# Splitting the first weight load of a transfer-bound decode kernel: 8 KB runs first, 24 KB runs last

## The chip, the cores and the metric

The kernel runs on one core of one Trainium2 chip. The metric is the device time of one execution in microseconds (us), median of several. A "run" of bytes (8 KB runs) is a contiguous stretch that a transfer moves as one packet; idle time in "engine-us" is summed over the sixteen DMA engines. The profile is one execution; its span is some 1.3 us shorter than the device time of the same execution. A "kernel before" always ran on the same chip beside the kernel it is compared with. Ratios are the mean time of one kernel's runs over that of the other's of the same rounds, so they are not quite the ratio of the medians quoted beside them.

## The reference

One decode step of an attention mixer beside an MLP, mixed by a gate, for batch 8, one token, width 576:

```
q = x @ wq                                  # wq: 576 x 4096, 32 heads of 128
k, v = the last 2048 of 8192 cached rows    # 16 kv heads, each used by two q heads
a = softmax(q k^T / sqrt(128)) v @ wo
b = gelu(layernorm(x) @ w1 + b1) @ w2 + b2
g = sigmoid(sum(x * gate_w))
out = g * a + (1 - g) * b
```

Nearly all of its work is reading: K and V are 67 MB each, the four weights 20 MB together.

## The kernel before

A plan lists all operations with what they depend on, a small cost model puts them in order for each engine, and that order is emitted. All large loads are issued by SP (SyncE) one after the other, in a fixed sequence. The parts that matter:

```python
# the first loads (SP), in this order; the weights wq and w1 share the K/V buffer slots
d_wqr = dma("sp", ... (wq_r, A_wq[512:576, :].rearrange("k (s c) -> (k s) c", s=2)), "wq", ...)       # 0.5 MB, 4 KB runs
d_wqm = dma("sp", ... (wq_m..., A_wq[0:512, :].rearrange("(p t) c -> p (t c)", t=4)), "wq", ...)      # 4.2 MB, 32 KB runs
dwq = [d_wqm, d_wqr]
d_w1m = dma("sp", ...)                                                                                # 4.7 MB, 36 KB runs
d_w1r = dma("sp", ...)                                                                                # 0.6 MB
# ... cut: q_fn multiplies xT by wq_m and wq_r and waits for dwq ...
# the sequence of the other loads: a number is a K load (4.2 MB), v a V load (2.1 MB), w wo, m w2
order = ("0 1 v 2 v 3 v 4 v v 5 v v 6 v v 7 v v 8 v v 9 v v 10 v v 11 v v 12 v v 13 v v 14 v 15 "
         "w w v v w w v v v v v v b m m m m")
# a K load waits until the K load two before it has been transposed (DVE), as it takes its buffer
slot_free[s] = trs
# ... cut ...
# at the end: the first two SP issues (and one of ACT) are moved ahead of the start barrier
for etype, count in ((mybir.EngineType.SP, 2), (mybir.EngineType.Activation, 1)):
```

Of the kernel before, what the change touches and what calls it, by code (L numbers as in the profile page):

```python
# [38 lines left out]
class _Plan:  # L39
# [16 lines left out]
    def dma(self, eng, fn, semkey, nbytes, deps=(), name=None, after=(), prio=0):  # L56
        op = _Op(eng, fn, deps, name, self.DMA_ISSUE, after=after, is_dma=True, dma_sem=semkey, nbytes=nbytes, prio=prio)
        op.idx = len(self.all)
        self.all.append(op)
        return op  # L60
# [108 lines left out]


ARENA_BASE = 16512


def held_matmul(nc, e, out, lhsT, rhs, start=False, stop=True, skip=False, tile_size=(128, 128), tile_position=(0, 0)):
    return e.add_instruction(mybir.InstMatmult(
        name=nc.get_next_instruction_name(), engine=mybir.EngineType.PE,
        ins=[e.lower_ap(rhs), e.lower_ap(lhsT)], outs=[e.lower_ap(out)],
        start_tensor_calc=start, stop_tensor_calc=stop, is_transpose=False, bass_skip_group_check=skip,
        tile_size=tile_size, tile_position=tile_position, ldweights=False))


def build_kernel(nc, A_x, A_k_cache, A_v_cache, A_wq, A_wo, B_x, B_w1, B_b1, B_w2, B_b2, gate_w, out):
# [24 lines left out]
    with ExitStack() as es:  # L207
# [126 lines left out]
        wq_m = RAW[:, WQO:WQO + 4 * 4096].rearrange("p (t c) -> p t c", t=4)  # L334
        wq_r = RAW[:, WQO + 4 * 4096:WQO + 4 * 4096 + 2048]
# [22 lines left out]
        add, dma = P.add, P.dma  # L358
# [26 lines left out]
        d_b1 = dma("act", lambda e: e.dma_start(b1c, B_b1.rearrange("(c f) -> c f", c=FC)), "b", F * 2, name="d_b1", after=[d_gw])  # L385
        dx = [d_x, d_gw, d_gw1]
        db = [d_b1]
        d_wqr = dma("sp", lambda e: e.dma_start(wq_r, A_wq[512:576, :].rearrange("k (s c) -> (k s) c", s=2)), "wq", 64 * 8192, name="d_wqr")
        d_wqm = dma("sp", lambda e: e.dma_start(wq_m.rearrange("p t c -> p (t c)"), A_wq[0:512, :].rearrange("(p t) c -> p (t c)", t=4)), "wq", 512 * 8192, name="d_wqm", after=[d_wqr])
        dwq = [d_wqm, d_wqr]  # L390
        d_w1m = dma("sp", lambda e: e.dma_start(w1_m.rearrange("p t c -> p (t c)"), B_w1[0:512, :].rearrange("(p t) c -> p (t c)", t=4)), "w1", 512 * F * 2, name="d_w1m", after=[d_wqm])
        d_w1r = dma("sp", lambda e: e.dma_start(w1_r, B_w1[512:576, :].rearrange("k (s c) -> (k s) c", s=2)), "w1", 64 * F * 2, name="d_w1r", after=[d_w1m])
        dw1 = [d_w1m, d_w1r]
# [173 lines left out]
        count = {"K": 0, "V": 0, "W": 0, "M": 0, "B": 0}  # L567
# [266 lines left out]
        handles = {"sp": nc.sync, "act": nc.scalar, "pool": nc.gpsimd, "dve": nc.vector, "pe": nc.tensor}  # L834
        for eng in ENGS:
            P.emit(eng, handles[eng], eng_sems, dma_sems)
        for etype, count in ((mybir.EngineType.SP, 2), (mybir.EngineType.Activation, 1)):
            first = [i for i in entry[n_entry:] if i.engine == etype][:count]
            assert all(isinstance(i, mybir.InstDMACopy) for i in first)
            for i in first:  # L840
                entry.remove(i)
            at = next(n for n, i in enumerate(entry) if i.engine == etype and isinstance(i, mybir.InstDrain))
            entry[at:at] = first
# [4 lines left out]
def bass_gated_mix__sliding_block_cached__mixer_channel_mlp__decode_kernel(  # L848
    nc: bass.Bass,
    A_x: bass.AP,  # L850
    A_k_cache: bass.AP,
    A_v_cache: bass.AP,
    A_wq: bass.AP,
    A_wo: bass.AP,
    B_x: bass.AP,
    B_w1: bass.AP,
    B_b1: bass.AP,
    B_w2: bass.AP,
    B_b2: bass.AP,
    gate_w: bass.AP,  # L860
    out: bass.AP,
):
    build_kernel(nc, A_x, A_k_cache, A_v_cache, A_wq, A_wo, B_x, B_w1, B_b1, B_w2, B_b2, gate_w, out)
# [28 lines left out]
```

## Time and profile before

| | kernel before |
|---|---|
| device time | 366.29 us (366.27 to 366.82, 3 runs) |
| span of the profile | 364.9 us |
| bytes read | 154.31 MB, 423 GB/s over the span |
| DMA queue of SP | 98.9% of sixteen DMA engines |
| DVE, PE busy | 62%, 66% |

The table says that the sixteen DMA engines are the bound: what does not make them start sooner, run faster or end more evenly does not show in the time. The lines themselves are in the prediction.

### The profile page before, as it was taken

The numbers are of one execution on the slowest core, as the hardware profiler recorded it, in microseconds if no ns is written. First come the engines' busy times: TensorE is split into PE (matmuls) and PEld (weight loads), VectorE is DVE, ScalarE is ACT, GpSimd is POOL, SyncE is SP. The second block draws the span as 40 slices with busy tenths as digits, with TensorE's granted clock in tenths as the row PEclk, the third lists the DMA queues.
The fourth block names the chain that finished last, engine by engine and source line by source line (L and its number), as shares of the span: only waits on it lengthen the run. The fifth ranks groups of instructions, "written<-read, shape, count | busy, mean of one in ns | idle before, by whom it ended". The sixth has DMA issues, their size and how long they took to land.

```text
span 364.9 us, 3980 instructions
## 1 busy us (share of the span) xinstructions
PE 239.4 (66%) x1679; PEld 115.0 (32%) x1679; DVE 226.5 (62%) x340; ACT 22.4 (6%) x53; POOL 17.4 (5%) x80
## 2 busy tenths in 40 slices
PE   0269684838498938274959484738959297577575
PEld 0159331312143414022423232214424133234232
DVE  4700995675999280759965362789781739777221
ACT  1010000000000000000100000001100000001000
POOL 5021000001000000010000000000000000000000
PEclk9999998778589969596996978676978796859899
DMA  9999999999999999999999999999999999999995
GB/s 376 435 404 451 406 451 411 451 432 415 445 426 443 420 436 431 424 438 424 436 426 440 422 442 420 439 422 438 424 436 444 426 410 436 425 431 429 431 425 222
DMA packets 9690, 154.58 MB, mean 424 GB/s; under 512 B 1052, under 2 KB 1220, under 8 KB 2888
## 3 DMA queue, kind: packets, MB, share of 16 engines
q1 hardware_dynamic: 9616, 154.29, 98.9%
q8 instruction: 13, 0.21, 0.2%
q10 hardware_dynamic: 56, 0.03, 0.0%
q14 instruction: 5, 0.04, 0.0%
HBM read 154.31 MB, written 0.01 MB: 423 GB/s over the span
## 4 chain that ended last, share of the span: by engine, by line
DMA 62%; DVE 24%; PE 11%; issue 1%; SPq 0%; DVEq 0%
DMA arena<-in_A_k_cache_dram 54%; DVE arena L666 18%; PE ps L678 6%; DMA arena<-in_A_v_cache_dram 5%; PE ps L711 4%; DMA arena<-in_B_w_dram 4%; DVE arena L639 3%; DVE arena L597 1%; DVE arena L631 1%; DVE arena L600 0%; DVE arena L606 0%; PE ps L612 0%; DVE arena L614 0%; PE ps L555 0%; SPq L798 0%
## 5 line engine op out<-in xcount | busy, mean ns | idle before, releaser
L666 DVE STREAM_TRANSPOSE arena<-arena 128x4096 f32<-128x4096 f32 x32 | 140.7, 4424 | 85.4 <-DMA arena<-in_A_k_cache_dram 85.0
L678 PE MATMUL ps<-arena 128*32 128x512 bf16 x512 | 141.7, 440 | 62.7 <-DVE arena L666 62.7
L678 PEld LDWEIGHTS ps<-arena 128*32 128x32 bf16 x512 | 52.3, 105 | 144.7 <-DVE arena L666 67.7
L711 PE MATMUL ps<-arena 128*32 128x512 bf16 x512 | 60.7, 453 | 23.8 <-DVE arena L602 18.6
L711 PEld LDWEIGHTS ps<-arena 128*32 128x32 bf16 x512 | 24.8, 110 | 50.4 <-issue 31.7
L639 DVE STREAM_TRANSPOSE arena<-arena 128x512 bf16<-128x512 bf16 x32 | 30.8, 1019 | 0.0
L728 PE MATMUL ps<-arena 128*128 128x16 f32 x128 | 17.0, 264 | 5.6 <-ACT arena L722 3.9
L761 DVE COPY arena<-arena 32x4 bf16<-32x4 bf16 (+1 forms) x80 | 12.9, 161 | 10.1 <-POOL arena L749 7.9
L728 PEld LDWEIGHTS ps<-arena 128*128 128x128 f32 x128 | 15.5, 191 | 11.5 <-ACT arena L722 9.6
L722 ACT ACTIVATE arena<-ps 128x512 f32<-128x512 f32 x16 | 9.6, 598 | 148.9 <-PE ps L711 148.9
L749 POOL TENSOR_TENSOR arena<-arena 128x8 bf16<-128x8 f32 x30 | 5.9, 231 | 229.9 <-ACT arena L738 229.9
L597 DVE TENSOR_REDUCE arena<-ps 128x1 f32<-128x512 f32 x8 | 5.5, 692 | 12.2 <-PE ps L678 12.1
L510 PE MATMUL ps<-arena 128*128 128x8 bf16 x144 | 10.9, 201 | 2.6 <-DMA arena<-in_B_w_dram 2.6
L608 ACT ACTIVATE arena<-ps,arena 128x512 bf16<-128x512 f32 x8 | 5.5, 687 | 107.4 <-DVE arena L606 107.4
L510 PEld LDWEIGHTS ps<-arena 128*128 128x128 bf16 x144 | 10.8, 157 | 3.1 <-DMA arena<-in_B_w_dram 3.1
L555 PE MATMUL ps<-arena 128*8 128x288 bf16 (+1 forms) x140 | 9.3, 288 | 3.6 <-DMA arena<-in_B_w_dram 3.4
L659 POOL TENSOR_TENSOR arena<-arena 128x32 bf16<-128x32 bf16 x32 | 6.5, 240 | 86.0 <-PE ps L678 76.9
L612 PE MATMUL ps<-arena 128*128 128x32 f32 x16 | 3.9, 328 | 8.6 <-DVE arena L611 8.6
L631 DVE TENSOR_SCALAR arena<-arena 128x512 bf16<-128x512 bf16 x32 | 9.0, 324 | 0.0
L425 PE MATMUL ps<-arena 8*128 8x8 bf16 x8 | 0.6, 170 | 11.0 <-DVE arena L398 7.0
L512 PE MATMUL ps<-arena 128*128 128x8 bf16 x36 | 7.2, 201 | 0.0
L555 PEld LDWEIGHTS ps<-arena 128*8 128x8 bf16 (+1 forms) x140 | 4.6, 85 | 7.8 <-DMA arena<-in_B_w_dram 4.9
(84 smaller groups left out, 77.8 us busy)
## 6 DMA issues: line engine op xcount, KB each, us to landing
arena<-in_A_k_cache_dram SPq DMA_DIRECT2D x16, 4096.0 KB, 25.2
arena<-in_A_v_cache_dram SPq DMA_DIRECT2D x32, 2048.0 KB, 24.3
arena<-in_B_w_dram SPq DMA_DIRECT2D x1, 4608.0 KB, 24.1
arena<-in_A_wo_dram SPq DMA_DIRECT2D x4, 1152.0 KB, 10.0
arena<-in_A_wq_dram SPq DMA_DIRECT2D x1, 4096.0 KB, 13.4
arena<-in_B_w_dram SPq DMA_DIRECT2D x3, 1296.0 KB, 18.9
arena<-in_B_w_dram SPq DMA_DIRECT2D x2, 432.0 KB, 12.2
arena<-in_B_w_dram SPq DMA_DIRECT2D x1, 576.0 KB, 25.2
```

Source lines behind the costliest of these rows:

```text
L510: ins = e.matmul(out_, lhsT, yT[:, kt, :], start=(kt == 0), stop=False)
L512: ins = e.matmul(out_, lhsT, yT[:, 4 + c // 2, :], start=False, stop=True)
L555: ins = e.matmul(ps[c:c + 8, BK_ACC, 0:JN], lhsT, rhs[:, JN * j:JN * j + JN], start=False, stop=True, skip_group_check=True, tile_position ...
L597: mx = add("dve", lambda e: e.tensor_reduce(out=k(MX), in_=ps[:, bank, :], axis=AXL.X, op=ALU.max), deps=[qk_done[g]], name="mx%d" % g, co ...
L631: return e.tensor_scalar(out=dst, in0=view("Pd").rearrange("p (s n) -> p s n", s=2), scalar1=amask[:, a:a + 1], scalar2=None, op0=ALU.mult)
L639: return e.transpose(dst, src)
L666: tr = add("dve", (lambda h=h, kb=kb: lambda e: e.transpose(bass.AP(arena_f, offset=foffs("KT") + kb * SE // 2, ap=[[AST // 2, 128], [4, 1 ...
L678: mm = e.matmul(ps[32 * c:32 * c + 32, 2 * (G % 2) + nb, :], qb[:, G % 2, n, 2 * h + ee, :], rhs, start=(h == 0 and t == 0), stop=(h == 1 ...
L711: mm = e.matmul(ps[c:c + 32, bk, :], PT[:, g % 2, 512 * q + 32 * t:512 * q + 32 * t + 32], slot(s)[:, 512 * t:512 * t + 512], start=(t < 2 ...
L722: u_ev[item] = add("act", lambda e: e.activation(out=EV[:, item % 2, :], in_=ps[:, bk, :].rearrange("p (r d j) -> p r j d", r=4, j=4), fun ...
L728: mm = e.matmul(ps[:, BK_S, OC + 16 * (item % 2):OC + 16 * (item % 2) + 16], EV[:, item % 2, 128 * r:128 * r + 128], i2[:, r, :, :].rearra ...
L761: return [add("dve", (lambda j=j, q=q: lambda e: e.tensor_copy(oT[32 * q:32 * q + 32, ch, j, bs], oN[32 * j:32 * j + 32, q, ch, bs]))(), d ...
```

## The change

The intent: let the first transfer carry more bytes for each descriptor, so that the DMA engines are fed sooner. The first load becomes one row in four of wq (1 MB in 8 KB runs), then comes the remainder of 64 rows, then the other three quarters in 24 KB runs. Three issues stand ahead of the start barrier, at which the engines wait for each other before they begin, in place of two. A helper that nothing called is removed.

```diff
-def held_matmul(nc, e, out, lhsT, rhs, ...):        (8 lines, cut)
...
-        d_wqr = dma("sp", lambda e: e.dma_start(wq_r, A_wq[512:576, :].rearrange("k (s c) -> (k s) c", s=2)), "wq", 64 * 8192, name="d_wqr")
-        d_wqm = dma("sp", lambda e: e.dma_start(wq_m.rearrange("p t c -> p (t c)"), A_wq[0:512, :].rearrange("(p t) c -> p (t c)", t=4)), "wq", 512 * 8192, name="d_wqm", after=[d_wqr])
-        dwq = [d_wqm, d_wqr]
+        wq_rows = A_wq[0:512, :].rearrange("(p t) c -> p t c", t=4)
+        d_wq0 = dma("sp", lambda e: e.dma_start(wq_m[:, 0, :], wq_rows[:, 0, :]), "wq", 128 * 8192, name="d_wq0")
+        d_wqr = dma("sp", ... as before ..., after=[d_wq0])
+        d_wqm = dma("sp", lambda e: e.dma_start(wq_m[:, 1:4, :].rearrange("p t c -> p (t c)"), A_wq[0:512, :].rearrange("(p t) c -> p (t c)", t=4)[:, 4096:16384]), "wq", 384 * 8192, name="d_wqm", after=[d_wqr])
+        dwq = [d_wqm, d_wqr, d_wq0]
...
-        for etype, count in ((mybir.EngineType.SP, 2), (mybir.EngineType.Activation, 1)):
+        for etype, count in ((mybir.EngineType.SP, 3), (mybir.EngineType.Activation, 1)):
```

More of the change, by code (lines that the diff above doesn't have):

```diff
@@ L171 @@
 ARENA_BASE = 16512
-def held_matmul(nc, e, out, lhsT, rhs, start=False, stop=True, skip=False, tile_size=(128, 128), tile_position=(0, 0)):
-    return e.add_instruction(mybir.InstMatmult(
-        name=nc.get_next_instruction_name(), engine=mybir.EngineType.PE,
-        ins=[e.lower_ap(rhs), e.lower_ap(lhsT)], outs=[e.lower_ap(out)],
-        start_tensor_calc=start, stop_tensor_calc=stop, is_transpose=False, bass_skip_group_check=skip,
-        tile_size=tile_size, tile_position=tile_position, ldweights=False))
 def build_kernel(nc, A_x, A_k_cache, A_v_cache, A_wq, A_wo, B_x, B_w1, B_b1, B_w2, B_b2, gate_w, out):
@@ L387, in build_kernel @@
         db = [d_b1]
-        d_wqr = dma("sp", lambda e: e.dma_start(wq_r, A_wq[512:576, :].rearrange("k (s c) -> (k s) c", s=2)), "wq", 64 * 8192, name="d_wqr")
-        d_wqm = dma("sp", lambda e: e.dma_start(wq_m.rearrange("p t c -> p (t c)"), A_wq[0:512, :].rearrange("(p t) c -> p (t c)", t=4)), "wq", 512 * 8192, name="d_wqm", after=[d_wqr])
-        dwq = [d_wqm, d_wqr]
+        wq_rows = A_wq[0:512, :].rearrange("(p t) c -> p t c", t=4)
+        d_wq0 = dma("sp", lambda e: e.dma_start(wq_m[:, 0, :], wq_rows[:, 0, :]), "wq", 128 * 8192, name="d_wq0")
+        d_wqr = dma("sp", lambda e: e.dma_start(wq_r, A_wq[512:576, :].rearrange("k (s c) -> (k s) c", s=2)), "wq", 64 * 8192, name="d_wqr", after=[d_wq0])
+        d_wqm = dma("sp", lambda e: e.dma_start(wq_m[:, 1:4, :].rearrange("p t c -> p (t c)"), A_wq[0:512, :].rearrange("(p t) c -> p (t c)", t=4)[:, 4096:16384]), "wq", 384 * 8192, name="d_wqm", after=[d_wqr])
+        dwq = [d_wqm, d_wqr, d_wq0]
         d_w1m = dma("sp", lambda e: e.dma_start(w1_m.rearrange("p t c -> p (t c)"), B_w1[0:512, :].rearrange("(p t) c -> p (t c)", t=4)), "w1", 512 * F * 2, name="d_w1m", after=[d_wqm])
```

## The prediction

> **What bounds the kernel now.** I read the page first, its slices and its queue table, then the chain that ended last, then the DMA queue's own waits, then the windows of the first and last microseconds.
>
> ```profile
> span 364.9 us, 3980 instructions
> ...
> DMA  9999999999999999999999999999999999999995
> GB/s 376 435 404 451 406 451 411 451 432 415 445 426 443 420 436 431 424 438 424 436 426 440 422 442 420 439 422 438 424 436 444 426 410 436 425 431 429 431 425 222
> ...
> q1 hardware_dynamic: 9616, 154.29, 98.9%
> ...
> DMA arena<-in_A_k_cache_dram 54%; DVE arena L666 18%; PE ps L678 6%; DMA arena<-in_A_v_cache_dram 5%; PE ps L711 4%; DMA arena<-in_B_w_dram 4%; DVE arena L639 3%; DVE arena L597 1%; DVE arena L631 1%; DVE arena L600 0%; DVE arena L606 0%; PE ps L612 0%; DVE arena L614 0%; PE ps L555 0%; SPq L798 0%
> ```
>
> The reader is to see that the transfers fill the span: the DMA row is 9 in every slice but the last, and the queue of the SP engine, which carries all the large loads, takes 98.9% of the sixteen DMA engines' time. DVE and PE show 62% and 66%. DVE stands on the chain only because the chain walks through the transposes that free a K buffer, and the loads that follow are already queued behind others. So the end is first byte + bytes at the engines' rate + tail. The windows give these three:
>
> ```profile
> 0.00:1.00 1.00, 0.00 (x0) 0.00 (x0) 0.00 (x0) 0.00 (x0) 0.20 (x4) 1.00 0.00 0
> 1.00:2.00 1.00, 0.00 (x0) 0.00 (x0) 0.36 (x6) 0.00 (x0) 0.70 (x3) 1.00 0.84 243
> 2.00:3.00 1.00, 0.00 (x0) 0.00 (x0) 0.92 (x3) 0.56 (x1) 0.98 (x7) 1.00 1.45 549
> ...
> 24.00:36.00 12.00, 9.40 (x153) 9.07 (x152) 0.00 (x0) 1.02 (x1) 3.21 (x16) 1.00 1.02 433
> ...
> 360.00:365.00 5.00, 2.21 (x30) 0.86 (x24) 0.45 (x1) 0.00 (x0) 0.00 (x0) 1.00 0.20 73
> ```
>
> The columns are the stretch, its length, the busy time of the engines, the granted clock, the DMA share and the GB/s. The last two count a packet where it falls, so one-microsecond shares can exceed 1. No byte moves in the first microsecond, the second one is weak, and from then on the rate is some 430 GB/s until 360. All that the change can touch lies in the first three microseconds. How much is queued there is in the order of time of the SP queue:
>
> ```profile
> 0.00 0.38 SPq L388 DMA_DIRECT2D arena<-in_A_wq_dram  x1
> 0.43 0.42 SPq L389 DMA_DIRECT2D arena<-in_A_wq_dram  x1
> 1.26 0.33 SPq L391 DMA_DIRECT2D arena<-in_B_w_dram  x1
> 1.64 0.65 SPq L392 DMA_DIRECT2D arena<-in_B_w_dram  x1
> 2.34 20.71 SPq L649 DMA_DIRECT2D arena<-in_A_k_cache_dram  x2
> ...
> 18.05 0.27 PE L472 MATMUL ps<-arena 128*128 128x8 bf16 x4
> ```
>
> By 2.9 us the kernel has issued 0.52 MB and 4.19 MB of wq, 4.72 and 0.59 MB of w1 and 4.19 MB of K: 14.2 MB. The packet records of the trace, summed, reach 13.8 MB at 34 us, so this queue lasts to about 35 us. The next K load waits for the q product (line 474) and is issued near 22.5 us, twelve microseconds before the queue could run dry. The q product itself starts at 18.05 us directly behind other PE work and not on a wait for wq, which landed at 0.43 + 13.4 = 13.8 us.
>
> **What the Trainium skill says.** Three places in its page "DMA: Bandwidth & Descriptors".
> - Section "Latency and other measured facts" puts the first byte of a transfer issued from SP at about 600 ns. The trace agrees: the first issue ends at 0.38 us and the first packet starts at 1.006 us, 0.63 us later.
> - Section "Why a DMA increments its semaphore by 16 and not by 1" says that 128 partitions spread over all 16 engines, and warns that transfers which share a semaphore are only safe to read at the full count. The three wq transfers share one, and the q product waits for all three, so this is neither a race nor a new wait. The trace agrees on the 16: there are 16 completion packets for each large load.
> - Section "Issuing engines are not separate DMA queues" says that more issues only save sequencer time, since all run on the same 16 engines. Here it means that an issue more on SP adds no bandwidth, and this kernel has no issue time to save after the first.
>
> **The change part by part.** I use the packet records, which no view lists one by one. Median durations on one engine: 4 KB 0.159 us, 16 KB 0.611 us, 32 KB 1.213 us. Two points give a line: (1213 - 611) ns for 16384 B is 27.2 B/ns, plus 9 ns of fixed time for each packet. So 8 KB should take 0.310 us and 24 KB 0.912 us (estimates from that line).
>
> (a) *Removed helper.* It is called nowhere in the kernel: 0 us.
>
> (b) *Smaller packets.* Before, each engine moved eight 32 KB packets of the main part: 8 x 1.213 = 9.70 us. After, it moves eight of 8 KB and eight of 24 KB: 8 x (0.310 + 0.912) = 9.78 us. That is 8 fixed times of 9 ns, +0.07 us. The remainder of 64 rows keeps its 4 KB packets: 0. The third transfer adds one completion packet of 9 ns per engine and about 6 ns between: +0.02 us. Sum +0.09 us, all on the path, since the engines are busy without a break afterwards.
>
> (c) *The start.* This is the intent. Before, an engine begins with eight 4 KB packets; at 0.159 us they would be done 1.27 us after the first packet, at 2.28 us. In the records the sixteen completion packets of that first transfer start between 2.54 and 3.16 us, at 2.9 us in the mean: 0.6 us lost for each engine. I split it. True idle time, with the packets' time taken from sixteen engines, is 0.21 us in the second microsecond and 0.06 in the third: the engine waits for its next descriptor. Slow first packets (280 to 620 ns instead of 159) come to (24.9 us summed over 128 packets)/16 - 1.27 = 0.28 us. The rest, about 0.1 us, are packets of x and gate_w on the ACT queue. Afterwards the first eight packets are of 8 KB. If descriptors arrive at the same pace, each covers twice the time, so I expect most of the 0.27 us of idle to go, say 0.15 to 0.25 us. The slow first packets are a latency that I take as unchanged in number, and the ACT packets stay. Gain -0.20 us.
>
> (d) *The issue order.* Three issues now stand ahead of the start barrier in place of two. The third costs SP about 0.42 us (the row of 0.43 us), and if SP's arrival (0.85 us) is what let the other engines go at 1.26 us, everything behind the barrier starts up to 0.4 us later. That is x, the gate, q and the w1 issues. The w1 load then comes at about 1.7 us, with 4.7 MB (11 us) of wq before it; q ends at 22.8 in place of 22.4 us, 12 us before the queue is dry. On the path: 0.
>
> (e) *The plan of the kernel.* Order on the engines comes from a cost model in the kernel, which sees the same bytes in the same sequence; I read no changed tie that matters. 0.
>
> Sum: +0.09 - 0.20 = -0.11 us, on 366.29: **366.2 us**.
>
> **The rivals.** First, *the start is pure latency*: the 0.6 us are memory and descriptor latency which a larger packet does not hide, so only (b) is left. For it: nearly half of the loss are slow packets, not idle engines. Against it: 0.27 us of measured idle. It would give 366.4 us.
>
> Second, *the first transfer of 4 KB runs was far worse than I count*, and 8 KB runs start at full rate at once. The cumulated bytes are 0.567 MB at 3 us, 1.69 us behind a stream at 432 GB/s from time zero; 1.0 us of that is before the first packet, so no more than 0.69 us can be won. It would give 366.29 - 0.69 + 0.09 = 365.7 us. Against it: the packets that run in the middle of that transfer take 159 ns, near the full rate.
>
> Third, *a new wait*: the later barrier and a different interleaving of gate_w between the packets delay the gate chain, which starts only when gate_w lands at about 10 us, so that q and the next K issue come late. For it: gate_w took over 8 us to land. Against it: the 12 us of slack. A delay of a few microseconds still changes nothing; it would need the q product beyond 32 us, and then each microsecond more would be one lost. I give that 1%.
>
> Fourth, *the tail decides*. The sixteen engines do not end together: completion packets of the last load lie between 360.9 and 362.2 us, and the window from 360 on shows only 0.20 of the DMA share. Which engine is last may change with the start by a few tenths, in either direction.
>
> **Range and chances.** The three times of before are 366.27, 366.29 and 366.82, so one run in three lies half a microsecond up without any change. With the mechanisms between -0.6 and +0.1 us, and tail and repeat of some 0.4 us, 365.6 to 366.9 us should hold it 8 times in 10. Two per cent are 7.3 us, more than ten times all that stands in the first three microseconds, so within 2% is nearly certain: 0.98, with 0.01 on each side.
>
> **What would show it.** Right: in the windows of after, still nothing before 1 us; more bytes through 3 us than 0.79 MB (the windows' own count, 243 + 549 kB); idle of the engines between 1 and 3 us reduced from 0.27 us to 0.1; the K load lands 0.1 us earlier than at 36.62 us; the page again 9 everywhere at about 154.3 MB, with 1024 + 16 completion packets and 128 packets more. The w1 issue moves from 1.26 to about 1.7 us without an effect on the end. Wrong: a first packet later than 1.1 us, 8 KB packets slower than 0.31 us in their middle, a gap before the 24 KB packets, or a K load issued after the queue has gone idle. Each would show as a lower share in the first four windows, and only the last could cost more than a microsecond.

## More of the kernel before

```profile
q8 instruction: 13, 0.21, 0.2%
```

Beside the data, thirteen packets of 16 KB fetch instructions, each on one of the sixteen engines. They look negligible.

## The result, and the profile after

The changed kernel took 366.93 us (366.34 to 366.99, 4 runs) and the kernel before 366.49 us (366.27 to 366.82, 4 runs); the ratio is 1.0008, with a 95% interval of 0.999 to 1.0025. That is "same" at 2%, and not clear of noise. A later series of runs resolved it better (e1 and e2 below): 0.5 to 0.6 us slower.

The page of the changed kernel, the same parts as those shown of before in the prediction (slices, SP's queue, the chain by line):

```profile
span 365.6 us, 3981 instructions
...
DMA  9999999999999999999999999999999999999994
GB/s 376 458 408 428 425 427 428 436 438 410 452 410 442 421 439 430 423 450 418 448 414 446 414 452 412 445 418 448 412 446 418 450 401 439 424 429 428 429 426 190
...
q1 hardware_dynamic: 9760, 154.29, 98.7%
...
DMA arena<-in_A_k_cache_dram 54%; DVE arena L660 20%; PE ps L672 5%; DMA arena<-in_A_v_cache_dram 5%; DMA arena<-in_B_w_dram 3%; DVE arena L633 3%; PE ps L705 2%; DVE arena L625 1%; DVE arena L591 1%; DVE arena L594 0%; DVE arena L600 0%; DVE arena L608 0%; SPq L792 0%; PE ps L549 0%; DVE arena L605 0%
```

The same bytes, 144 packets more (128 of data and 16 of completion, as predicted). The last slice shows 190 in place of 222 GB/s: the difference is in the tail. The windows of the same stretches as before:

```profile
0.00:1.00 1.00, 0.00 (x0) 0.00 (x0) 0.00 (x0) 0.00 (x0) 0.20 (x4) 1.00 0.00 0
1.00:2.00 1.00, 0.00 (x0) 0.00 (x0) 0.12 (x2) 0.00 (x0) 0.27 (x1) 1.00 0.95 241
2.00:3.00 1.00, 0.00 (x0) 0.00 (x0) 0.68 (x6) 0.30 (x1) 0.94 (x6) 1.00 0.99 407
```

These columns end in DMA share and GB/s. The second microsecond is no better than before (241 against 243 GB/s), and the third shows less (407 against 549; the view counts a packet whole where it starts). The two together are 0.65 MB, where the prediction wanted more than 0.79 MB as a sign of its gain. The order of time on the SP queue, with the start of the q product:

```profile
0.90 0.43 SPq L383 DMA_DIRECT2D arena<-in_A_wq_dram  x1
1.74 0.33 SPq L385 DMA_DIRECT2D arena<-in_B_w_dram  x1
...
17.26 0.27 PE L466 MATMUL ps<-arena 128*128 128x8 bf16 x4
```

The third wq issue stands at 0.90 us and the barrier opens at 1.7 us in place of 1.26 us; the q product starts 0.8 us earlier than before (18.05), since the small b1 load, on which a PE transpose ahead of it waits, happened to land 0.8 us earlier (that transpose starts at 11.87 us, before at 12.68). None of that is on the path.

Where the time went is in the chain that ended last. Two pieces of it for the kernel before (start, duration, what; the first K load and the last w2 load):

```profile
2.34 34.28 DMA arena<-in_A_k_cache_dram
...
349.35 12.86 DMA arena<-in_B_w_dram
```

and for the changed kernel:

```profile
2.63 33.83 DMA arena<-in_A_k_cache_dram
...
350.16 12.76 DMA arena<-in_B_w_dram
```

Start plus duration is the landing. The first K load lands at 36.46 us in place of 36.62, 0.16 us earlier, as if the start had been won. The last load lands at 362.92 us in place of 362.21, 0.71 us later. So 0.87 us were lost between 36 and 363 us, in a stretch that the change does not touch. The packet records of the trace, which no view lists one by one, show two places.

**At 49 to 52 us some engines run dry.** The third K load waits for two DVE transposes of the first one. Its issue on the SP queue, in the kernel before and in the changed kernel:

```profile
45.81 0.54 SPq L649 DMA_DIRECT2D arena<-in_A_k_cache_dram  x1
```

```profile
45.65 0.54 SPq L643 DMA_DIRECT2D arena<-in_A_k_cache_dram  x1
```

The loads ahead of it end on the first engine at 49.1 us in the changed kernel (before: 49.3 us). In the changed kernel four engines sat idle for 370 to 650 ns until 49.7 us, up to 4.1 us after the issue, and the first packets of several took 100 to 470 ns longer than 1213 ns. Summed over sixteen engines the idle time from 48.5 to 52 us was 1.93 engine-us; in the kernel before it was 0.59. Elsewhere between 26.5 and 340 us neither kernel had any.

**At the end one engine is late.** Its last data packet ended at 362.90 us, that of the next at 362.23. In the kernel before the last two ended at 362.17 and 362.15.

### The profile page after: what moved, and what is told of

The parts are those of the page before. It is cut to its first block, busy times and chain, and to the rows that moved or that the text cites. A ratio compares the mean times of both kernels' runs of the same rounds, so it can differ in the third digit from the quotient of the medians. Undisturbed runs are those within 1.5% of the kernel's fastest.

```text
span 365.6 us, 3981 instructions
## 1 busy us (share of the span) xinstructions
PE 236.9 (65%) x1679; PEld 114.3 (31%) x1679; DVE 226.4 (62%) x340; ACT 22.4 (6%) x53; POOL 17.4 (5%) x80
## 3 DMA queue, kind: packets, MB, share of 16 engines
q1 hardware_dynamic: 9760, 154.29, 98.7%
## 4 chain that ended last, share of the span: by engine, by line
DMA 63%; DVE 26%; PE 8%; issue 1%; SPq 0%; DVEq 0%
DMA arena<-in_A_k_cache_dram 54%; DVE arena L660 20%; PE ps L672 5%; DMA arena<-in_A_v_cache_dram 5%; DMA arena<-in_B_w_dram 3%; DVE arena L633 3%; PE ps L705 2%; DVE arena L625 1%; DVE arena L591 1%; DVE arena L594 0%; DVE arena L600 0%; DVE arena L608 0%; SPq L792 0%; PE ps L549 0%; DVE arena L605 0%
## 5 line engine op out<-in xcount | busy, mean ns | idle before, releaser
L672 PE MATMUL ps<-arena 128*32 128x512 bf16 x512 | 139.0, 434 | 64.5 <-DVE arena L660 64.5
L705 PE MATMUL ps<-arena 128*32 128x512 bf16 x512 | 61.3, 454 | 25.4 <-DVE arena L596 18.7
L549 PE MATMUL ps<-arena 128*8 128x288 bf16 (+1 forms) x140 | 10.1, 294 | 3.3 <-DMA arena<-in_B_w_dram 3.3
```

Of the source, the lines that this page charges most:

```text
L549: ins = e.matmul(ps[c:c + 8, BK_ACC, 0:JN], lhsT, rhs[:, JN * j:JN * j + JN], start=False, stop=True, skip_group_check=True, tile_position ...
L672: mm = e.matmul(ps[32 * c:32 * c + 32, 2 * (G % 2) + nb, :], qb[:, G % 2, n, 2 * h + ee, :], rhs, start=(h == 0 and t == 0), stop=(h == 1 ...
L705: mm = e.matmul(ps[c:c + 32, bk, :], PT[:, g % 2, 512 * q + 32 * t:512 * q + 32 * t + 32], slot(s)[:, 512 * t:512 * t + 512], start=(t < 2 ...
```

## The experiments

Two theories to begin with. **A**: a lead won at the start is lost again near 49.7 us, and where the starving hits an engine that is late at the end, that sets the time. **B**: the tail is only noise. Each had five rounds (five runs, six for e6 and e12). They ran in three groups of four; a group shares a chip and the runs of the kernel before. The three groups ran on three different chips, whose kernels before had medians of 366.19 (e1 to e4), 366.44 (e5 to e8) and 366.38 us (e9 to e12).

### e1: the kernel before, again

No edit.

> The kernel before, unchanged, for a second profile and more times. Theory A (a lead won at the start is lost again near 49.7 us, where the queue runs nearly dry before the third K load, and what is lost there on the engine that ends last decides the end): the first K load lands at 36.6 us as before; some idle time of the DMA engines between 49 and 51 us (0.03 us in the mean of the engines in the first profile, 0.12 us in that of the changed kernel); where an engine that later ends last starves there, the run is near 366.9 us, else near 366.3. Theory B (only noise of the tail, nothing at 49.7 us matters): times scatter between 366.2 and 367.0 without a relation to idle time at 49 us.

Measured: 366.31 us (366.05 to 366.45), ratio 1.0003. Its profile shows no idle at all at 49 us and two engines level at the end (361.98 and 362.04 us). The first K load landed at 36.48 us, as early as in the changed kernel: the 36.62 of the first profile was chance.

### e2: the changed kernel, again

No edit.

> The changed kernel, unchanged. Theory A: first K load lands at 36.46 us again, 0.1 to 0.2 us before the kernel before; idle of 0.1 us in the mean at 49 to 50 us again; times mostly near 366.9 with some at 366.3, ratio 1.000 to 1.002. Theory B: the landing is 0.1 to 0.2 us earlier in this one too, and the time is 0.1 us less in the mean over five rounds, ratio 0.9995.

Measured: 366.78 us (366.62 to 366.89), ratio 1.0015 (1.0003 to 1.0028). Its five times lie above all fourteen of the kernel before from e1 and its neighbours on the same chip (366.05 to 366.45), so the loss is real, and B's 0.1 us gain is not there. Idle near 49.7 us again: 1.29 engine-us; the last engine at 362.76, the next at 362.06. The landing of the first K load, 36.60 us, was not earlier.

### e3: the kernel before, with one V load moved ahead

```diff
-        order = ("0 1 v 2 v 3 v 4 ...
+        order = ("0 1 v v 2 3 v 4 ...
```

> The kernel before with one change in the order of the large loads: the second V load (2 MB) is issued ahead of the third K load, so that the queue holds about 4.9 us more work at 46 us. Order on all other engines is unchanged. Theory A: no idle time of the DMA engines between 45 and 55 us (below 0.01 us in the mean), the fan of the engines does not open there, and all runs are near 366.2 us or below. Theory B: times as the kernel before, 366.3 to 366.9. Against both: if the later third K load stalls the transposes, the time rises by more than 1 us.

Measured: 366.21 us (366.10 to 366.59), ratio 1.0003. No idle at 49 us. As the kernel before had hardly starved, there was little to win. Theory A's "all runs near 366.2 us" did not hold: two of the five took 366.56 and 366.59, without a profile, so runs half a microsecond longer occur with this order too.

### e4: the changed kernel, with the same V load moved ahead

The edit of e3 on the changed kernel.

> The changed kernel with the same reordering. Theory A: the lead won at the start is kept past 50 us: at 100 us the DMA engines have 0.1 to 0.2 us less lost time than the kernel before with this reordering, and the run is 0.1 to 0.2 us below it, near 366.0 us; it is 0.3 to 0.8 us below the changed kernel. Theory B: no different from the changed kernel.

Measured: 366.17 us (366.11 to 366.36), ratio 0.9999. All five runs lie below all five of e2. No idle at 49 us, and the last engines end at 362.16 and 362.06 us. The SP queue in e4 (start, us, line, count) shows the edit, two V loads queued long before the third K load:

```profile
22.32 16.02 SPq L691 DMA_DIRECT2D arena<-in_A_v_cache_dram  x2
45.70 10.40 SPq L643 DMA_DIRECT2D arena<-in_A_k_cache_dram  x2
```

The third K load is issued no earlier than before; it only has 4.9 us of other work ahead of it. That one edit takes the idle time and the loss away together, so the loss goes with the dry queue. The edit also places all later loads differently against the instruction fetches, and no run separates the two. e4 comes out at e3's time (366.17 and 366.21): theory A's 0.1 to 0.2 us between them did not appear, though the runs of one kernel scatter by more than that. The windows of the tail, for the kernel before, the changed kernel, and e4 (columns as before):

```profile
360.00:362.30 2.30, 1.60 (x26) 0.73 (x22) 0.00 (x0) 0.00 (x0) 0.00 (x0) 1.00 0.41 154
362.30:363.00 0.70, 0.61 (x6) 0.13 (x6) 0.05 (x1) 0.00 (x0) 0.00 (x0) 1.00 0.00 0
```

```profile
360.00:362.30 2.30, 1.69 (x26) 0.95 (x28) 0.00 (x0) 0.00 (x0) 0.00 (x0) 1.00 0.42 155
362.30:363.00 0.70, 0.52 (x8) 0.17 (x10) 0.00 (x0) 0.00 (x0) 0.00 (x0) 1.00 0.05 20
```

```profile
360.00:362.30 2.30, 1.66 (x26) 0.72 (x23) 0.00 (x0) 0.00 (x0) 0.00 (x0) 1.00 0.37 134
362.30:363.00 0.70, 0.59 (x6) 0.11 (x6) 0.06 (x1) 0.00 (x0) 0.00 (x0) 1.00 0.00 0
```

After 362.3 us nothing moves in the kernel before and in e4. In the changed kernel 5% of the engines still do, and one engine of sixteen is 6%: a single engine holds up the end.

### e5: no new start, but one large load more

Why do the engines starve with the change? Two candidates: **L**, the lead won at the start makes the queue run dry sooner; **R**, one more load in the queue makes the third K load's descriptors come later. The edit splits another load of the kernel before:

```diff
-        d_w1m = dma("sp", ... w1_m (36 KB runs) ..., after=[d_wqm])
+        d_w1a = dma("sp", ... w1_flat[:, 0:2 * F] (18 KB runs) ..., after=[d_wqm])
+        d_w1m = dma("sp", ... w1_flat[:, 2 * F:4 * F] (18 KB runs) ..., after=[d_w1a])
```

> The kernel before with its w1 main load cut into two loads of 18 KB runs: the start is untouched, one large load more stands in the queue ahead of the third K load, as in the changed kernel. Theory R (what starves the engines at 49.7 us is the one load more in the queue, not the lead): idle of 0.08 us or more in the mean of the engines between 49 and 51 us, time 366.7 to 367.0, ratio 1.001 to 1.002. Theory L (the lead won at the start makes the queue run dry before the third K load arrives): no lead here, so no idle at 49.7 us beyond 0.03 us, time 366.2 to 366.4.

Measured: 366.97 us (366.39 to 367.32), ratio 1.0014 (1.0002 to 1.0026). The time is R's, but the profile, which fell on the run of 366.39, shows no idle. Neither theory is borne out; see e9.

### e6: the 32 KB load first

```diff
-        d_wqr = dma("sp", ... 4 KB runs ...)
-        d_wqm = dma("sp", ... 32 KB runs ..., after=[d_wqr])
+        d_wqm = dma("sp", ... 32 KB runs ...)
+        d_wqr = dma("sp", ... 4 KB runs ..., after=[d_wqm])
```

> The kernel before with the two wq loads exchanged: the 4 MB load in 32 KB runs comes first, the remainder of 64 rows second; the number of loads and packets is that of the kernel before. The start: if idle for want of descriptors is what costs there, the lost time up to 3 us is smaller than in the kernel before (1.19 to 1.27 us so far) by 0.1 to 0.2 us, and the first K load lands near 36.45 us. Theory R: no starving at 49.7 us, time 366.0 to 366.3. Theory L: starving at 49.7 us as in the changed kernel, 366.7 to 366.9.

Measured: 366.58 us (366.46 to 368.01, 6 runs), ratio 1.0012 (1.0000 to 1.0024), with no idle at 49 us. The start was not better: time without a packet up to 3 us, the first microsecond included, was 1.29 us of a mean engine, against 1.27 and 1.19 in the two profiles of the kernel before. Neither R's 366.0 to 366.3 us nor L's starving came. What its 0.12% comes from I have not found; its last engine ends at 362.56 us, 0.15 after the next.

### e7: the changed kernel with the barrier as before

```diff
-        for etype, count in ((mybir.EngineType.SP, 3), ...
+        for etype, count in ((mybir.EngineType.SP, 2), ...
```

> The changed kernel with only its first two wq loads ahead of the start barrier, as before: the other engines start 0.47 us earlier and the third wq load is issued behind the barrier at about 1.3 us. If the later barrier is the cause of the added 0.6 us: 366.2 us. Theories R and L both: starving at 49.7 us and 366.7 to 366.9, as in the changed kernel, unless the third load comes too late for the engines, which would cost up to 0.3 us more at the start.

Measured: 366.81 us (366.27 to 367.12), ratio 1.0011 (0.9998 to 1.0024, so the time alone is not clear of noise), idle 1.93 engine-us at 49.7 us. It starves as the changed kernel does, so the later barrier is not needed for it.

### e8: the kernel before with the later barrier

```diff
-        for etype, count in ((mybir.EngineType.SP, 2), ...
+        for etype, count in ((mybir.EngineType.SP, 3), ...
```

> The kernel before with three issues ahead of the start barrier (its two wq loads and the w1 load): the barrier opens near 1.7 us in place of 1.26 us, all else is unchanged. If the later barrier is the cause: 366.7 to 366.9 us. Theories R and L: no starving, 366.2 to 366.4 us as before.

Measured: 366.30 us (366.20 to 366.50), ratio 0.9998 (0.9986 to 1.0009), idle 0.05 engine-us. The barrier opened at 1.73 us and cost nothing. With e7 this clears the barrier in both directions.

### e9: e5 again

No edit to e5.

> The kernel before with its w1 load in two parts, a second time, for a second profile: the first one fell on the fastest of its five runs (366.39) and shows no starving, while the other four took 366.8 to 367.3. Theory R (one large load more in the queue ahead of the third K load makes the descriptors of that load reach some engines late, so that they starve): the median is again 0.3 to 0.7 us above the kernel before, and a profile that falls on a slow run (366.8 or more) shows over 1 engine-microsecond of idle near 49.7 us. If a slow run shows none, R is wrong for this kernel and the cause of its excess is another.

Measured: 366.41 us (366.24 to 366.52), ratio 1.0000, no idle near 49.7 us. On this chip the extra load cost nothing, and in neither of its two profiles did it starve the engines. Yet it has as many packets on SP's queue as the changed kernel (9760). R in its plain form falls. What made e5 slow on the other chip is open, as none of its slow runs has a profile.

### e10: e5 with the V load moved ahead

The edits of e5 and e3 together.

> The same with the second V load ahead of the third K load. Theory R: 366.2 to 366.5 us, as near the kernel before as the changed kernel came with this reordering, 0.4 us or more below the split kernel without it. If the split costs by its 8 further packets and one completion per engine alone: 0.1 us above the kernel before, with and without reordering.

Measured: 366.35 us (366.16 to 366.60), ratio 1.0000. No difference from e9: where nothing starves, the reordering wins nothing.

### e11: the changed kernel without the remainder's load

```diff
-        d_wqr = dma("sp", ... wq_r, 4 KB runs ...)
-                ins = e.matmul(out_, wq_r[:, c * 128:(c + 1) * 128], xT[:, 4 + hq // 16, :], ...)
+                ins = e.matmul(out_, wq_m[:, 0, c * 128:(c + 1) * 128], xT[:, 4 + hq // 16, :], ...)
```

The number of issues ahead of the barrier goes back to two. The result is wrong.

> The changed kernel without the load of the remaining 64 rows of wq; the q product reads other wq rows in their place, so its result is wrong on purpose. It keeps the split start in 8 KB and 24 KB runs and has as many loads ahead of the third K load as the kernel before, and moves 0.52 MB less, 1.2 us at the measured rate. Theory R (the number of loads): no starving at 49.7 us later shifted to about 48.5 us, time near 366.3 - 1.2 = 365.1 us. Theory S (something in the split wq loads themselves): over 1 engine-microsecond of idle at that place, time near 365.6 us.

Measured: 364.86 us (364.79 to 365.06), ratio 0.9960. All moves 1.3 us earlier, so I looked from 47 to 50.5 us: 0.61 engine-us of idle, as in the first profile of the kernel before, and no late engine (360.96 and 360.89). The time is 1.5 us below the kernel before on that chip (366.38); the bytes left out explain 1.2 us by the estimate, the rest is not explained. The split start alone, with as many loads as before, does not starve as the changed kernel does. So neither an extra load alone (e5, e9) nor the split alone does it.

### e12: the changed kernel with e5's split too

The edit of e5 on the changed kernel.

> The changed kernel with the w1 load in two parts too, so two loads more than the kernel before ahead of the third K load. Theory R: starving at 49.7 us at least as strong as in the changed kernel (1.3 to 1.9 engine-microseconds of idle), 366.8 to 367.3 us. Theory S, or no effect of the number: as the changed kernel, 366.7 to 367.0.

Measured: 366.36 us (366.15 to 367.74, 6 runs), ratio 1.0006. The profile fell on the run of 367.74: 2.45 engine-us of idle, the most of all, and one engine ends at 363.69 us, 1.5 us after the next. The other five runs took 366.15 to 366.77, about as the kernel before on that chip (365.94 to 366.66), so the median bears out neither R nor S. Whether these five starved is not known, as they have no profile. The changed kernel itself did not run on this chip, so its loss is clear of noise on one chip only (e2).

### All profiled executions

The third column sums idle time of the sixteen engines from 48.5 to 52 us (e11: 47 to 50.5), from the packet records.

| kernel | third K issue, us | idle, engine-us | last engine ends, next | device time of that execution |
|---|---|---|---|---|
| before | 45.81 | 0.59 | 362.17, 362.15 | 366.21 |
| e1 before again | 45.67 | 0.00 | 362.04, 361.98 | 366.05 |
| e8 later barrier | 45.67 | 0.05 | 362.22, 362.12 | 366.30 |
| e5 w1 split | 45.94 | 0.00 | 362.38, 362.28 | 366.39 |
| e9 w1 split again | 46.17 | 0.00 | 362.44, 362.38 | 366.41 |
| e6 32 KB first | 45.69 | 0.00 | 362.56, 362.41 | 366.50 |
| changed | 45.65 | 1.93 | 362.90, 362.23 | 366.90 |
| e2 changed again | 45.79 | 1.29 | 362.76, 362.06 | 366.78 |
| e7 changed, barrier as before | 45.86 | 1.93 | 362.59, 362.42 | 366.61 |
| e12 changed, w1 split | 45.87 | 2.45 | 363.69, 362.18 | 367.74 |
| e3 before, V ahead | (after V) | 0.00 | 362.19, 362.11 | 366.21 |
| e4 changed, V ahead | (after V) | 0.00 | 362.16, 362.06 | 366.17 |
| e10 w1 split, V ahead | (after V) | 0.00 | 362.16, 362.14 | 366.25 |
| e11 without remainder | 44.49 | 0.61 | 360.96, 360.89 | 364.97 |

The four executions that starve by more than 1 engine-us are the four of the changed start with all its three loads and the old order, and they are the four slowest of the full-size kernels. The margin does not tell them apart: from the issue of the third K load to the end of the work ahead on the first engine it was 3.19 us in e12, which starved most, and 3.18 us in e9, which did not starve.

**How 0.4 us on an early engine could become 0.6 us at the end.** In the mean of sixteen engines, 1.93 engine-us of idle are only 0.12 us, so the end must hang on single engines. Each large load gives every engine the same share (eight packets of each K load), and in these records an engine that fell behind did not catch up: in the kernel before, the gap between the first and the last engine to complete a load was 0.6 us for the first load, 1.5 us at 49 us and 2.8 us at 340 us. It grew mostly in steps that follow instruction fetches, such as from 1.83 to 2.73 us after the one at 251.4 us, and stayed level between. The Trainium skill, "Runtime: NRT & Kernel Launch", section "Instruction fetch mechanics", says that instructions are refilled in blocks of 16 KiB through a DMA queue of the sequencer; the trace agrees, with 13 packets of 16,384 B on queue q8, each 0.88 to 1.0 us long. The page calls their cost mostly hidden; here a data load beside it paid: near the fetch at 83 us one engine falls back by some 1.4 us. In the kernel before that engine had been among the first, and the fetch put it level with the others at the back (completions of the load at 89.48 and 89.54 us). In the changed kernel the engine hit at 84 us came from some 0.8 us further back, where the starving at 49.7 us had put it, and stood alone (89.34, then 90.30). At 345 us the last two completions were 344.57 and 345.52 us, in the kernel before 344.71 and 344.76.

The records carry no engine number. Up to 92 us, chaining the packets by their start and end times shows that the engine hit at 84 us is one of the four that starved; after some 300 us the chaining is no longer unique, so that it is also the one late at the end is argued, not shown. And it is the path of one profile, perhaps of e12 too, not of e2: there the last two completions were level at 89 us (89.46 and 89.47) and at 345 us (344.69 and 344.69), and yet its last engine ended 0.7 us after the next. How the starving reaches the end is therefore open in general. That the loss vanishes together with the starving (e4) is shown, on one chip.

## Why the prediction was right or wrong

**The class was right, the direction was not.** 366.2 us were predicted and 366.93 measured, within 2% and just above the range (365.6 to 366.9). A gain of 0.11 us stood in the sum; a loss came out, 0.4 us in the first result, where it is not clear of noise, and 0.6 us in e2. That the class was right says nothing for the mechanism: 2% are 7.3 us, ten times what the prediction itself saw in reach of the change, and what did cost time lay outside its sum.

**Step (a)**, the helper: nothing, as the equal order of instructions shows.

**Step (b)**, smaller packets: the estimates of 0.310 and 0.912 us for 8 KB and 24 KB packets were right; their medians are 0.309 and 0.912 us. The +0.09 us is too small to be seen in the time.

**Step (c)**, the start, is the step that failed. It took idle engines between 1 and 3 us as want of descriptors, and expected 8 KB packets to fill it. The first sixteen packets were slow at every size: a median of 0.295 us for 4 KB in the kernel before, 0.624 us for 8 KB in the changed kernel and 1.779 us for 32 KB in e6, against 0.159, 0.309 and 1.213 us later on. (Over all profiles the medians scatter, from 0.174 to 0.544 us for 4 KB and from 0.624 to 0.766 us for 8 KB.) The idle time from 1 to 3 us, counted as in the prediction, was 0.16 to 0.23 us with the new start (changed, e2, e4, e7) and 0.19 to 0.56 us with the old one, and never came down to the 0.1 us that was to show the gain. So the bytes moved by 3 us stayed the same: 0.56, 0.58, 0.55 and 0.55 MB in the four profiles with the old start (before, e1, e3, e8), 0.58, 0.52, 0.53 and 0.52 MB with the new one (changed, e2, e4, e7), 0.50 MB with 32 KB first. By 44 us the means are 18.091 and 18.112 MB; the difference of 0.021 MB is 0.05 us at 432 GB/s, and the old start alone scatters by 0.10 MB. The first rival, that the start is latency which a larger packet does not hide, fits this part; that it is latency was not measured apart. The landing of the K load 0.16 us earlier, which I had named as proof of the gain, was scatter: it came at 36.62 and 36.48 us with the old start, 36.46 and 36.60 with the new one.

**Step (d)**, the order of issue: the barrier moved by 0.47 us, about as predicted (0.4), and cost nothing that e8 shows. Its detail that q would end 0.4 us later was wrong, as q came after the b1 load, and that landed earlier; with so much slack it did not matter. Its reasoning had a hole: it followed the queue to the second K load, issued 12 us before the queue could run dry, and took that slack for all later loads. The third K load has 3.2 to 3.5 us between its issue and the end of the work ahead on the first engine, in both kernels, and in the changed kernel its first packets started on some engines only up to 4.1 us after the issue. That is where its engines starve, a term that the sum did not have.

**Step (e)**, no tie in the plan changes: right, by the comparison of the two programs.

**The rivals.** The third, a new wait that makes a K load come late, came nearest, but looked for it at the second K load behind the gate chain, and gave it 1%. The wait was at the third K load and short, and that load was issued 3.4 us before the queue ran dry. The prediction's signs of being wrong were looked for at the start, or in a K load issued after the queue had gone idle, and none of them covers this case. The fourth, the tail, was right that the last engine decides and may change by some tenths, but took it for chance; in e2 the loss was repeatable, five runs of five.

**What stays open.** Why the third K load's packets come later with the changed start. Not the barrier (e7, e8), not a lead (none was won, and the margin at the issue is the same), not one load more as such (e5, e9), not the split as such (e11). Only all three wq loads together starve by more than 1 engine-us, in four profiles of four (the kernel before reached 0.59 in one of two). How the starving becomes the late engine of e2. And why e5 was slower on one chip and not on another.

No version here beats the kernel before: e4 and e3 are level with it.

## What to carry to other kernels

When the DMA queue is the bound, look for its thinnest point over the whole run, the load with the least work queued between its issue and its first packet, and not only at the start; here one independent load moved ahead of it took the changed kernel's loss away (e4). Read the tail by the last engine, not by the mean: with equal shares on sixteen engines a delay on one of them was not made up by the others here. And repeat the profile of the kernel before, since a landing 0.16 us earlier, in one profile each, was no gain at all.

## What the Trainium skill lacked or had wrong

- "DMA: Bandwidth & Descriptors", section "Latency and other measured facts", gives a first-byte latency of about 600 ns. That held for the first load of all (0.63 us after its issue). It lacks two cases. A load issued while others still run: here some engines had its first packet only up to 4.1 us after the issue and sat idle until then (changed kernel, 45.65 to 49.7 us), so that a margin of 3.4 us was not enough. And the first packets of an execution, which were slower than later ones of the same size: in the median of sixteen 0.174 to 0.544 us for 4 KB (seven profiles), 0.624 to 0.766 us for 8 KB (six) and 1.779 us for 32 KB (one), against 0.159, 0.309 and 1.213 us later.
- "Runtime: NRT & Kernel Launch", section "Instruction fetch mechanics", calls the cost of a 16 KiB refill mostly hidden. It gives no figure for what a refill costs the data loads beside it: 0.88 to 1.0 us on one of the sixteen engines for each of thirteen, and an engine hit near 83 us fell back by 1.4 us.
